# Taking absolute values of float64 weight words on ScalarE two pieces ahead and on VectorE, with the cells of steps 2 and 3 in another hand order

## Chip, cores and metric

The kernel runs on one core of a Trainium2 chip. The metric is the time of one execution on the device in microseconds (us). Engines are called PE (TensorE), DVE (VectorE), ACT (ScalarE), POOL (GpSimd) and SP (SyncE, which only issues transfers here).

## What is computed

An mLSTM cell runs over 4 batches x 8 heads x 768 positions with a head size of 40, and its output (3072 tokens x 320) goes through a feed-forward block: `h = x @ w_in` (320 x 2048), `g = max(0.01 h, h)`, `out = g @ w_out` (2048 x 320).

```python
m_new = maximum(f + m, i);  C = exp(f + m - m_new) * C + exp(i - m_new) * v k^T   # per head, per position
h = C q;  y = sigmoid(o) * h / max(|n q|, 1)
g = maximum(0.01 * (x @ w_in), x @ w_in);  out = g @ w_out
```

The two weight matrices come in as float64 and have to be narrowed to float32 on the core. q, k, v and the gates are float32.

## The kernel before

**Tiling.** The 768 positions are cut into 6 chunks of 128. A *step* `s` is one chunk of one batch (24 steps, chunk `s // 4`, batch `s % 4`). The *cell* of a step consists of a few functions, each of which issues the work of several engines: `u_transpose` (k and q transposed on PE, copied to `kqT` by ACT from step 2 on, L331), `u_scores` (PE `sc` L340, then two DVE multiplications L344), `u_state` (PE `pc` L354 and `dC` L365), `u_values` (PE `pa` L384, then on DVE the denominators L389 to L393), `gate` (DVE L402, then POOL L405, which gives `x`), and `u_x` (PE transposes `x`, ACT copies it to `xT`). `prep_exp` holds eight exponentials on ACT (L301), `prep_o` a tanh on ACT (L316), `prep_mask` a POOL addition (L291), `prep_vu` a POOL multiplication (L309).

**Feed-forward.** `ff_units(g)` gives the feed-forward of chunk `g` as a list of units. For chunk 0 these are 8 units of `half` over the first 256 columns of `xT` (call them ff0 to ff7), 8 over the second 256, and 16 of `part`, which multiply by `w_out` (PE `po`, L474). A `half` unit is 8 matmul records at L430, 4 at L436, and two activations on ACT (L444). Unit ff*j* needs piece *j* of `w_in`. The 16 `part` units go in four rounds, one unit per batch each: round 0 needs pieces 8 and 9, round 1 pieces 10 and 11, and so on.

**Narrowing.** Each matrix is cut into 8 pieces of 128 x 640 values: pieces 0 to 7 are `w_in`, 8 to 15 `w_out`. `load_weights` brings a piece as 64-bit words into a buffer `raw` (6 of them). `narrow_weights(n)` then makes float32 of it: the absolute value of the high word (ACT, L155, in `absolute`), and six DVE instructions, L170, L174, L178, L180, L182 and L189. The high word is read with a stride of 8 bytes. It is a generator which yields after each DVE instruction, and `narrow(k)` issues the next `k` of them, whatever piece they belong to.

**Where the absolute value is issued.** For piece 0 and for every piece of `w_out` it comes right ahead of that piece's own L170; for pieces 1 to 7 it comes ahead of L189 of the piece before.

**What sets the order.** On PE, DVE, ACT and POOL the order of the instructions is the order in which the program issues them (`manual_schedule`): each engine works through its own queue, and waits at an instruction until its inputs are there. `first_chunk` is an order written by hand, with calls of `narrow` between cells and units. After it, a loop runs over the units of chunk 0 that are left (i = 0 to 23) and spreads the cells of chunk 1 between them from i = 6 on; from i = 4 on it calls `narrow(3)` ahead of each unit. At i = 5 it issues `u_gates(1)` and `ahead(4)` (POOL, ACT and POOL work for step 4), at i = 6 `gates(2)` (six DVE instructions L206 to L226, then ACT L219 and L220). On the SP queue a scheduler picks the order of the transfers.

Of the kernel before, what the change touches and what calls it, by code (L numbers as in the profile page):

```python
# [13 lines left out]
ALU = mybir.AluOpType  # L14
# [4 lines left out]
def kernel(  # L19
# [26 lines left out]
    nc = tc.nc  # L46
# [66 lines left out]
    NP = NF // 2  # L113
# [39 lines left out]
    def absolute(n):  # L153
        lo, hi, dst = raws[n]
        nc.scalar.activation(dst, hi.bitcast(F32), AF.Abs)  # L155

    def narrow_weights(n):

        if not wide:
            return
        if n == 0 or n >= NP:
            absolute(n)
        lo, hi, dst = raws.pop(n)
        mt = wk.tile([P, dst.shape[1]], U32, name="wm", bufs=1)
        m = mt[:]
        d = dst.bitcast(U32)

        nc.vector.tensor_scalar(  # L170
            m.bitcast(F32), dst, scalar1=2.0**-15, scalar2=122879.9921875, op0=ALU.max, op1=ALU.min,
        )
        yield
        nc.vector.tensor_scalar(  # L174
            m, m, scalar1=0x07FFFFFF, scalar2=3, op0=ALU.bitwise_and, op1=ALU.logical_shift_left,
        )
        yield
        nc.vector.scalar_tensor_tensor(d, in0=hi, scalar=0xC0000000, in1=m, op0=ALU.bitwise_and, op1=ALU.bitwise_or)  # L178
        yield
        nc.vector.tensor_scalar(m, d, scalar1=0xFF800000, scalar2=None, op0=ALU.bitwise_and)  # L180
        yield
        nc.vector.scalar_tensor_tensor(  # L182
            m.bitcast(F32), in0=lo, scalar=2.0**-52, in1=m.bitcast(F32), op0=ALU.mult, op1=ALU.mult,
        )
        yield
        if n + 1 < NP:

            absolute(n + 1)
        nc.vector.tensor_tensor(dst, dst, m.bitcast(F32), op=ALU.add)  # L189
        yield  # L190

# [101 lines left out]
    def prep_exp(s):  # L293

        c, b = divmod(s, B)
        if c == 0:
            w = st[s]["w"] = wk.tile([P, H, P], F32, name="w", bufs=NL)
        w = st[s]["w"]
        for h in range(H):
            bh = b * H + h  # L300
            nc.scalar.activation(w[:, h, :], w[:, h, :] if c > 0 else st[s]["ab"][h], AF.Exp, bias=gT[:, c, 0, bh : bh + 1], scale=1.0)  # L301
# [12 lines left out]
    def prep_o(s):  # L314

        nc.scalar.activation(st[s]["o"][:], st[s]["o"][:], AF.Tanh, scale=0.5)  # L316


    def u_transpose(s):
        d = st[s]  # L320
        d["kqT"] = wk.tile([P, 2, PR, P], F32, name="kqT")
        for i in range(2):
            tp = psc.tile([P, PR, P], F32, name="tkq", tag="c")
            for j in range(PR):
                nc.tensor.transpose(  # L325
                    tp[:, j, :], d["kq"][:, i, 2 * j : 2 * j + 2, :].rearrange("p h d -> p (h d)"), ident[:],
                )
            if s < 2:
                nc.vector.tensor_copy(d["kqT"][:, i], tp[:])
            else:  # L330
                nc.scalar.copy(d["kqT"][:, i], tp[:])  # L331

    def u_scores(s):
        d = st[s]
        kqT, w = d["kqT"], d["w"]
        sc = [psc.tile([P, PR, P], F32, name=f"sc{r}", tag="c") for r in range(2)]
        for j in range(PR):
            for r in range(2):
                rows = slice(DP * r, DP * r + D)
                nc.tensor.matmul(  # L340
                    sc[r][:, j, :], lhsT=kqT[rows, 0, j, :], rhs=kqT[rows, 1, j, :], start=True, stop=True,
                )
        for r in range(2):
            nc.vector.tensor_tensor(w[:, r::2, :], w[:, r::2, :], sc[r][:], op=ALU.mult)  # L344
# [52 lines left out]
    def gate(s):  # L397

        d = st[s]
        d["x"] = wk.tile([P, Dm], F32, name="x")  # L400
        x3 = d["x"][:].rearrange("p (h d) -> p h d", d=D)
        nc.vector.scalar_tensor_tensor(  # L402
            x3, in0=d["o"][:], scalar=1.0, in1=d["hn"][:, :, :D], op0=ALU.add, op1=ALU.mult,
        )
        nc.gpsimd.tensor_tensor(x3, x3, d["den"][:].unsqueeze(2).to_broadcast([P, H, D]), op=ALU.mult)  # L405

    def u_x(s):

        c, b = divmod(s, B)
        d = st[s]  # L410
        if b == 0:
            st["xT", c] = wk.tile([P, KF + 1, GT], F32, name="xT")
        xT = st["xT", c]
        xt = psc.tile([P, KF + 1, P], F32, name="xt", tag="c")
        for kk in range(KF):
            nc.tensor.transpose(xt[:, kk, :], d["x"][:, ts(kk, P)], ident[:])  # L416
        nc.tensor.transpose(xt[:KR, KF, :], d["x"][:, KF * P :], ident[:])
        nc.scalar.copy(xT[:, :KF, ts(b, P)], xt[:, :KF, :])
        for r in range(2):
            nc.scalar.copy(xT[KR * r : KR * (r + 1), KF, ts(b, P)], xt[:KR, KF, :])  # L420
        del st[s]
# [100 lines left out]
    def narrow(count):  # L522
        for _ in range(count):
            next(narrowing, None)

    def first_chunk():

        load(0)
        load(1)
        load_weights(0)  # L530
        load_o(0)
        load_o(1)
        for n in range(1, 5):
            load_weights(n)
        load(2)
        load_weights(5)
        load_weights(6)
        load_weights(7)
        load(3)
        load_o(2)  # L540
        load_o(3)
        load_weights(NP)
        load_weights(NP + 1)
        ab = mask_first((0, 1), (0, 1, 2, 3))
        bu, a = gates(0)
        gates_T(0, bu)
        spread_first(a, ab, (0, 1))
        prep_exp(0)
        u_transpose(0)
        prep_vu(0)  # L550
        u_scores(0)
        prep_exp(1)
        u_state(0)
        u_transpose(1)
        prep_vu(1)
        u_values(0)
        u_scores(1)
        u_state(1)
        narrow(2)
        prep_o(0)  # L560
        gate(0)
        narrow(1)
        u_values(1)
        prep_o(1)
        gate(1)
        narrow(3)
        u_x(0)
        u_x(1)
        ffs = ff_units(0)
        ffs[0]()  # L570
        narrow(6)
        ab = mask_first((2,), (0, 2))
        spread_first(a, ab, (2,))
        ffs[1]()
        prep_exp(2)
        narrow(6)
        ffs[2]()
        narrow(6)
        ab = mask_first((3,), (0, 2))
        spread_first(a, ab, (3,))  # L580
        ffs[3]()
        prep_exp(3)
        narrow(6)
        u_transpose(2)
        prep_vu(2)
        ffs[4]()
        u_scores(2)
        narrow(3)
        u_state(2)
        narrow(3)  # L590
        u_values(2)
        ffs[5]()
        prep_o(2)
        narrow(3)
        gate(2)
        u_transpose(3)
        prep_vu(3)
        narrow(3)
        u_x(2)
        u_scores(3)  # L600
        ffs[6]()
        narrow(3)
        u_state(3)
        u_values(3)
        prep_o(3)
        gate(3)
        narrow(3)
        ffs[7]()
        u_x(3)
        return ffs[8:]  # L610

    E = mybir.EngineType
    with tc.manual_schedule(engines={E.PE, E.DVE, E.Activation, E.Pool}):
        ffs = first_chunk()
        bus[1] = gates(1)
        feed(B)
        load_weights(NP + 2)
        load_weights(NP + 3)
        feed(B + 1)
        load_weights(NP + 4)  # L620
        load_weights(NP + 5)
        feed(B + 2)
        load_weights(NP + 6)
        load_weights(NP + 7)
        feed(B + 3)
        for c in range(1, NB + 1):
            if c > 1:
                ffs = ff_units(c - 1)
            cells = cell_units(c) if c < NB else []
            n_ff, n_c = len(ffs), len(cells)  # L630
            lead = 6 if c == 1 else 0
            done = 0
            for i in range(n_ff):
                if c == 1 and i >= 4:
                    narrow(3)
                if c == 1 and i == 5:
                    u_gates(1)
                    ahead(B)
                if i == lead and c + 1 < NB:
                    bus[c + 1] = gates(c + 1)  # L640
                ffs[i]()
                upto = min(n_c, max(0, i + 1 - lead) * n_c // (n_ff - 3 - lead))
                while done < upto:
                    fn, s = cells[done]
                    fn(s)
                    done += 1
                    if fn is u_transpose:
                        ahead(s + 1)
                    elif fn is u_values and s + NL < NS:
                        feed(s + NL)  # L650
# [31 lines left out]
```

## Time and profile before

| | |
|---|---|
| three timed runs | 641.93, 640.20, 641.08 us (median 641.08) |
| the profiled execution | span 641.0 us, mean granted PE clock 0.963 |
| PE busy | 610.6 us, 95% of the span |
| DVE, ACT, POOL busy | 177.9, 184.7 and 102.1 us |
| L155 on ACT | 16 times, about 0.79 us each |

The page gives one execution. A row such as `L474 PE MATMUL po<-w_out,act ... x768 | 224.6, 444` reads: 768 instructions of line 474, 224.6 us in all, 444 ns each on average. PE's share of 95% is an average over a start in which PE waits and a long rest in which it doesn't, so the stages have to be looked at apart.

### The profile page before, as it was taken

Reading aid. Unit: us, or ns where it says so; the run is one execution under the profiler, and the core shown is the slowest. Engines: PE = TensorE matmul, PEld = TensorE weight load, DVE = VectorE, ACT = ScalarE, POOL = GpSimd, SP = SyncE. Lnnn points to the kernel's source line nnn. Section 1 sums busy time; section 2 is a strip of 40 time slices with the busy share of each in tenths; the row PEclk is TensorE's granted clock in tenths of the full one; section 3 lists DMA queues with packets and bytes.
Section 4 is the critical chain, followed back from the end, with each engine's and each line's share of the span. In section 5 each row is a group of like instructions: output and inputs, shape, how many; then the busy total and the mean of one; then the engine's idle time right before and its main releaser. Section 6 shows DMA issues by size and latency. Waiting matters only on the chain.

```text
span 641.0 us, 7844 instructions
## 1 busy us (share of the span) xinstructions
PE 610.6 (95%) x3062; PEld 388.7 (61%) x3062; DVE 177.9 (28%) x367; ACT 184.7 (29%) x505; POOL 102.1 (16%) x110
## 2 busy tenths in 40 slices
PE   8888697988899999999999999999999999999997
PEld 5656565766655557755557755557754467743475
DVE  4774606687622111222111222111201111100000
ACT  4333335322342341232441232441222441012200
POOL 3200112323122022022022021022011010000000
PEclk9597899897999999999999999999999999999999
DMA  9996442433233023133123122123120000000000
GB/s 166 235 214 174 97 170 66 102 75 65 42 86 72 13 64 77 46 70 59 26 63 77 44 70 56 30 64 75 43 61 2 0 1 15 17 11 0 1 20 21
DMA packets 112692, 41.51 MB, mean 65 GB/s; under 512 B 101424, under 2 KB 105936, under 8 KB 112656
## 3 DMA queue, kind: packets, MB, share of 16 engines
q1 hardware_dynamic: 112368, 40.79, 27.7%
q8 instruction: 24, 0.39, 0.2%
q10 hardware_dynamic: 288, 0.23, 0.2%
q14 instruction: 12, 0.10, 0.1%
HBM read 37.00 MB, written 4.01 MB: 64 GB/s over the span
## 4 chain that ended last, share of the span: by engine, by line
PE 84%; DVE 8%; ACT 4%; POOL 2%; issue 1%; POOLq 0%; DVEq 0%; ACTq 0%
PE po L474 29%; PE ph L430 27%; PE ph L436 8%; PE pa L384 7%; PE sc L340 4%; PE tkq L325 3%; PE pc L354 2%; ACT w L301 2%; PE dC L365 1%; PE ab L267 1%; DVE wm L182 1%; POOL w L291 1%; PE xt L416 1%; DVE w L344 1%; DVE w_in L189 1%
## 5 line engine op out<-in xcount | busy, mean ns | idle before, releaser
L474 PE MATMUL po<-w_out,act 128*128 128x320 f32 x768 | 224.6, 444 | 3.2 <-DVE w_out L189 3.2
L430 PE MATMUL ph<-xT,w_in 128*128 128x512 f32 (+1 forms) x448 | 190.4, 563 | 8.1 <-DVE w_in L189 7.2
L474 PEld LDWEIGHTS po<-w_out,act 128*128 128x128 f32 x768 | 143.3, 193 | 59.8 <-DVE w_out L189 4.2
L430 PEld LDWEIGHTS ph<-xT,w_in 128*128 128x128 f32 x448 | 84.3, 201 | 77.2 <-issue 59.3
L444 ACT ACTIVATE act<-ph 128x512 f32<-128x512 f32 (+1 forms) x112 | 53.9, 534 | 175.6 <-PE ph L436 175.6
L405 POOL TENSOR_TENSOR x<-x,den 128x320 f32<-128x320 f32 x24 | 18.6, 773 | 421.5 <-DVE x L402 421.5
L344 DVE TENSOR_TENSOR w<-w,sc 128x512 f32<-128x512 f32 x48 | 30.8, 683 | 186.9 <-PE sc L340 186.9
L436 PE MATMUL ph<-xT,w_in 64*128 64x512 f32 (+1 forms) x224 | 58.0, 595 | 0.0
L384 PEld LDWEIGHTS pa<-va,w 128*128 128x128 f32 x384 | 50.2, 207 | 10.3 <-issue 5.2
L384 PE MATMUL pa<-va,w 128*128 128x41 f32 x384 | 51.0, 295 | 2.5 <-DVE w L344 2.4
L479 ACT COPY y<-po 128x320 f32<-128x320 f32 x24 | 10.2, 423 | 147.1 <-PE po L474 85.2
L301 ACT ACTIVATE w<-w,gT 128x128 f32<-128x128 f32 x160 | 49.0, 399 | 11.4 <-POOL w L291 8.8
L291 POOL TENSOR_TENSOR w<-w,cmask 128x1024 f32<-128x1024 f32 x20 | 48.5, 2425 | 9.2 <-DMA w<-a_dr 9.2
L331 ACT COPY kqT<-tkq 128x512 f32<-128x512 f32 x44 | 23.7, 597 | 77.2 <-PE tkq L325 77.2
L436 PEld LDWEIGHTS ph<-xT,w_in 64*128 64x128 f32 x224 | 17.5, 191 | 36.8 <-issue 36.8
L340 PEld LDWEIGHTS sc<-kqT 40*128 40x128 f32 x384 | 24.4, 193 | 16.7 <-ACT kqT L331 8.8
L340 PE MATMUL sc<-kqT 40*128 40x128 f32 x384 | 28.6, 289 | 5.9 <-ACT kqT L331 5.0
L386 DVE TENSOR_TENSOR hn<-hn,pa 128x328 f32<-128x328 f32 x20 | 9.9, 496 | 70.0 <-PE pa L384 70.0
L325 PEld LDWEIGHTS tkq<-ident,kq 128*128 128x128 f32 x192 | 21.9, 143 | 11.4 <-issue 9.8
L358 DVE TENSOR_TENSOR hn<-pc,gT 128x328 f32<-128x328 f32 x20 | 10.0, 498 | 58.6 <-PE pc L354 58.6
L325 PE MATMUL tkq<-ident,kq 128*128 128x128 f32 x192 | 26.1, 280 | 0.0
L354 PEld LDWEIGHTS pc<-C,kqT 128*128 128x128 f32 x160 | 20.8, 192 | 7.0 <-issue 5.1
(70 smaller groups left out, 333.5 us busy)
## 6 DMA issues: line engine op xcount, KB each, us to landing
w<-a_dr SPq DMA_DIRECT2D x20, 512.0 KB, 5.0
raw<-in_moe_w_out_dram SPq DMA_DIRECT2D x8, 640.0 KB, 5.0
raw<-in_moe_w_in_dram SPq DMA_DIRECT2D x16, 256.0 KB, 4.2
kq<-in_k_dram SPq DMA_DIRECT2D x24, 160.0 KB, 2.8
kq<-in_q_dram SPq DMA_DIRECT2D x24, 160.0 KB, 3.3
va<-in_v_dram SPq DMA_DIRECT2D x24, 160.0 KB, 2.8
o_sb<-in_o_gate_dram SPq DMA_DIRECT2D x24, 160.0 KB, 4.6
out_dram<-y SPq DMA_DIRECT2D x24, 160.0 KB, 1.8
```

Source lines behind the costliest of these rows:

```text
L291: nc.gpsimd.tensor_tensor(w[:], w[:], cmask[:].unsqueeze(1).to_broadcast([P, H, P]), op=ALU.add)
L301: nc.scalar.activation(w[:, h, :], w[:, h, :] if c > 0 else st[s]["ab"][h], AF.Exp, bias=gT[:, c, 0, bh : bh + 1], scale=1.0)
L325: nc.tensor.transpose(tp[:, j, :], d["kq"][:, i, 2 * j : 2 * j + 2, :].rearrange("p h d -> p (h d)"), ident[:],)
L331: nc.scalar.copy(d["kqT"][:, i], tp[:])
L340: nc.tensor.matmul(sc[r][:, j, :], lhsT=kqT[rows, 0, j, :], rhs=kqT[rows, 1, j, :], start=True, stop=True,)
L344: nc.vector.tensor_tensor(w[:, r::2, :], w[:, r::2, :], sc[r][:], op=ALU.mult)
L354: nc.tensor.matmul(pc[:, 2 * j : 2 * j + 2, :].rearrange("p h d -> p (h d)"), lhsT=d["kqT"][:, 1, j, :], rhs=C[:, b, j].rearrange("p h d - ...
L384: nc.tensor.matmul(pa[:, h, :], lhsT=d["w"][:, h, :], rhs=d["va"][:, h, :], start=True, stop=True)
L430: nc.tensor.matmul(ph[:, cols], lhsT=w_full(kk, f), rhs=xT[:, kk, cols], start=(kk == 0), stop=False,)
L436: nc.tensor.matmul(ph[r][:, cols], lhsT=w_rest(r, j), rhs=xT[KR * r : KR * (r + 1), KF, cols], start=False, stop=True,)
L444: nc.scalar.activation(acts[f][:, cols], ph[r][:, cols], AF.Prelu, alpha=0.01)
L474: nc.tensor.matmul(po[n][:], lhsT=acts[f][:, ts(n, P)], rhs=w_out[:, f, :], start=(f == 0), stop=(f == NF - 1),)
```

## The change

Three edits, all of them in the narrowing and in the hand order:

1. For `w_in`, the absolute value of piece n + 2 is now issued ahead of L189 of piece n (before: piece n + 1), and that of piece 1 between L174 and L178 of piece 0. It stays on ACT.
2. For `w_out` the absolute value is now a DVE instruction, a bitwise AND with 0x7FFFFFFF on the high word, and a step of its own: a piece of `w_out` has seven steps in place of six. The loop calls `narrow(4)` in place of `narrow(3)`.
3. In `first_chunk`, the cells of steps 2 and 3 and the calls of `narrow` stand in another order.

```diff
-        if n == 0 or n >= NP:
-            absolute(n)
+        if n == 0:
+            absolute(0)
...
+        if n >= NP:
+            nc.vector.tensor_scalar(d, hi, scalar1=0x7FFFFFFF, scalar2=None, op0=ALU.bitwise_and)
+            yield
...
+        if n == 0:
+            absolute(1)
         nc.vector.scalar_tensor_tensor(d, in0=hi, scalar=0xC0000000, in1=m, op0=ALU.bitwise_and, op1=ALU.bitwise_or)
...
-        if n + 1 < NP:
-
-            absolute(n + 1)
+        if n + 2 < NP:
+
+            absolute(n + 2)
         nc.vector.tensor_tensor(dst, dst, m.bitcast(F32), op=ALU.add)
...
-        narrow(3)
+        narrow(2)
         u_x(0)
         u_x(1)
+        narrow(1)
         ffs = ff_units(0)
...
         narrow(6)
         ffs[2]()
-        narrow(6)
         ab = mask_first((3,), (0, 2))
         spread_first(a, ab, (3,))
-        ffs[3]()
-        prep_exp(3)
         narrow(6)
         u_transpose(2)
         prep_vu(2)
+        ffs[3]()
+        prep_exp(3)
+        narrow(3)
+        u_scores(2)
+        narrow(3)
+        u_state(2)
+        u_values(2)
         ffs[4]()
-        u_scores(2)
-        narrow(3)
-        u_state(2)
-        narrow(3)
-        u_values(2)
+        prep_o(2)
+        narrow(3)
+        gate(2)
+        narrow(3)
         ffs[5]()
-        prep_o(2)
-        narrow(3)
-        gate(2)
+        u_x(2)
         u_transpose(3)
         prep_vu(3)
         narrow(3)
-        u_x(2)
         u_scores(3)
+        narrow(3)
+        u_state(3)
         ffs[6]()
         narrow(3)
-        u_state(3)
         u_values(3)
         prep_o(3)
+        narrow(3)
         gate(3)
-        narrow(3)
         ffs[7]()
         u_x(3)
...
                 if c == 1 and i >= 4:
-                    narrow(3)
+                    narrow(4)
```

In the order of the compiled program, the PE instructions from the end of ff2 on to ff8, the first unit of the second half, stand like this:

| | order on PE |
|---|---|
| before | step 3's mask, ff3, transpose 2, ff4, scores 2, state 2, values 2, ff5, transpose 3, x 2, scores 3, ff6, state 3, values 3, ff7, x 3, ff8 |
| after | step 3's mask, transpose 2, ff3, scores 2, state 2, values 2, ff4, ff5, x 2, transpose 3, scores 3, state 3, ff6, values 3, ff7, x 3, ff8 |

After ff8 PE's order is the same in both. POOL's order is the same throughout. On DVE the w_out pieces 8 to 15 have eight instructions more, and with four steps ahead of each unit in place of three they stand earlier against the cells. On ACT eight L155 are gone from the part after ff8. On SP a few transfers change places with their neighbours (the loads of w_out pieces 10 to 14 and of the steps 4 to 8); none is added and none taken away.

More of the change, by code (lines that the diff above doesn't have):

```diff
@@ L585, in first_chunk @@
         prep_vu(2)
-        ffs[4]()
+        ffs[3]()
+        prep_exp(3)
+        narrow(3)
         u_scores(2)
@@ L589, in first_chunk @@
         u_state(2)
-        narrow(3)
         u_values(2)
-        ffs[5]()
+        ffs[4]()
         prep_o(2)
@@ L595, in first_chunk @@
         gate(2)
+        narrow(3)
+        ffs[5]()
+        u_x(2)
         u_transpose(3)
```

## The prediction
> **What bounds the kernel now.** I read the slices of the page first (PE's clock and share fall below 9 tenths only among the first eleven of 40), then cut the span into four stages: up to ff8, up to the end of scores 4, up to the transposes of x 7, and the rest. Busy time of each engine by stage, with the granted PE clock after it:
>
> ```profile
> core 0: us, PE busy (x) PEld busy (x) DVE busy (x) ACT busy (x) POOL busy (x), PEclk, DMA share, GB/s
> 0.00:84.80 84.80, 70.33 (x417) 49.02 (x417) 48.98 (x94) 29.27 (x86) 11.16 (x22) 0.80 0.79 178
> 84.80:112.70 27.90, 23.97 (x126) 17.09 (x126) 9.70 (x20) 13.18 (x41) 7.11 (x6) 0.95 0.37 111
> 112.70:176.70 64.00, 56.31 (x351) 43.03 (x350) 46.65 (x80) 19.37 (x53) 18.90 (x17) 0.91 0.33 70
> 176.70:641.00 464.30, 459.98 (x2170) 279.59 (x2170) 72.54 (x174) 122.84 (x327) 64.93 (x66) 1.00 0.18 41
> ```
>
> The last stage is PE at full clock without gaps, and the change touches nothing there: 464.3 us stay. Everything is decided in the first 177 us, where PE idles and runs at a reduced clock. Next the waits between 84 and 177 us (who waited for whom, sum, times, longest):
>
> ```profile
> DVE wm L170 <- ACT w_out L155: 29.9, 6, 15.4
> PE sc L340 <- ACT kqT L331: 3.9, 1, 3.9
> PE po L474 <- DVE w_out L189: 3.2, 2, 2.5
> ```
>
> DVE waits 29.9 us for absolute values on ACT that themselves take 0.79. Then the timeline (start, duration, engine, in brackets the idle time before and its releaser):
>
> ```profile
> 65.79 0.49 DVE L402 SCALAR_TENSOR_TENSOR x<-o_sb,pa 128x320 f32<-128x320 f32 x1 [3.81 <-ACT o_sb L316]
> 79.65 3.53 PE L430 MATMUL ph<-xT,w_in 128*128 128x256 f32 x8 [3.65 <-DVE w_in L189]
> 104.14 0.79 ACT L155 ACTIVATE w_out<-raw 128x640 f32<-128x640 f32 x1
> 104.96 0.50 DVE L170 TENSOR_SCALAR wm<-w_out 128x640 f32<-128x640 f32 x1 [4.05 <-ACT w_out L155]
> 108.48 0.40 ACT L219 ACTIVATE bu<-bu,a 32x128 f32<-32x128 f32 x1 [3.56 <-DVE bu L218]
> 110.60 2.15 PE L340 MATMUL sc<-kqT 40*128 40x128 f32 x16 [3.92 <-ACT kqT L331]
> 112.68 4.50 PE L474 MATMUL po<-w_out,act 128*128 128x320 f32 x8
> 120.37 2.40 PE L474 MATMUL po<-w_out,act 128*128 128x320 f32 x8
> 123.03 2.93 POOL L291 TENSOR_TENSOR w<-w,cmask 128x1024 f32<-128x1024 f32 x1
> 123.78 2.87 DVE L189 TENSOR_TENSOR w_out<-w_out,wm 128x640 f32<-128x640 f32 x1
> 134.79 1.34 PE L474 MATMUL po<-w_out,act 128*128 128x320 f32 x4 [2.50 <-DVE w_out L189]
> 150.16 0.41 PE L384 MATMUL pa<-va,w 128*128 128x41 f32 x2 [1.84 <-DVE w L344]
> ```
>
> The reader is to see a ring at 104 to 113: L155 stands on ACT behind the exponentials of step 4, DVE waits for it with gates(2) queued behind, ACT then waits for gates(2), the copy of kqT behind that is late, and PE idles 3.92 us. Scores 4 and the next eight `po` then run at half rate (2.15 for 1.16 us, 4.50 for 2.40). The last rows show the gaps of the third stage, and one thing to remember: an L189 of 0.82 us takes 2.87 beside a POOL mask.
>
> [...] ff5 runs slow at 59.78 (3.78) behind a gap of 0.83. [...] The trace: L170 0.49, L189 0.82 for the same 640 elements. [...]
>
> **The change part by part.** Start-to-start on DVE: 0.52 for L170, L174, L180 and 0.86 for L178, L182, L189, 4.1 a piece.
>
> *Removed and added.* Eight L155 leave ACT after ff8: 8 x 0.79 = 6.3 us, off the path except through DVE's waits. DVE gets eight ANDs. No row shows a tensor_scalar with an 8-byte stride; the bounds are L170 (0.49) and L178, which reads the same strided words at 0.82. I take 0.52; the other end adds 0.33 each, 2.6 in all. A cost below 0.49 is excluded, since L170 moves as many elements.
>
> *Stage 1, to ff8 (edits 1 and 3).* Up to 42.9 PE doesn't move: the masks of step 3 wait for the exponentials of step 2 (end 39.6) in both orders. Pieces 2 and 3 no longer wait for ACT (1.79 and 3.85 us of DVE idle): they run from 30.5 to 38.7, before: to 44.4. PE: transposes 2 to 43.8, ff3 (2.6) to 46.4 at full clock, scores 2 to 47.5. DVE: L344 twice to 48.9, the last three steps of piece 4 (2.2) to 51.1, where ff4 starts. Before, that first L344 pair ended at 55.7, so this is 6.8 us ahead. But the new order has ff5 behind ff4 with nothing between, and piece 5 stands on DVE behind gate(2), which needs a tanh that stands on ACT behind ff4's activations. Before, from such activations (64.74) over tanh, L402 and three steps to the next unit (69.27) took 4.5: ff4 ends at 53.8, ff5 starts at 58.3, with PE idle 4.5. At half rate ff5 takes 4.6 (62.9), x 2 and transposes 3 1.7, copies 1.1, scores 3 1.1, L344 1.3, three steps 2.2: ff6 at 70.3. It takes 4.3, pa 3 1.9 (76.5), denominators and three steps 2.8: ff7 at 79.3, before 79.65. The lead is spent on one more round of PE waiting for DVE waiting for PE: -0.4. If ff4 too runs at half rate (as ff5 did at 59.78; even odds) 2.8 come on top. I take **+1.0**; range -4.2 (ff5 and ff6 at full clock, 1.9 each) to +2.4.
>
> *Stage 2, ff8 to the first `po` (edit 2).* Piece 8 needs no ACT now: its seven steps fit into DVE's idle time after gates(1) (15.38 us before L170 at 96.5). So gT is copied when PE has it, at 98.2 instead of 100.6. Behind it stand four steps of piece 9 (2.4), the hold by step 5's mask (2.3, as with the 2.87) and gates(2) (1.6): 104.5. ACT: L219 and L220 0.7, activations 0.6, kqT 1.0: scores 4 at 106.8, where PE arrives at 106.3. Idle 3.9 becomes 0.5 (-3.4), scores 4 at full clock -1.0, the first `po` -2.1: **-6.5**; range -2 to -7.
>
> *Stage 3, to the transposes of x 7.* Losses of before: 2.50, 1.84 + 0.18 and 0.72 of idle, `pa` 6 slow (3.4 for 2.0), the `po` at 153.54 slow (4.54 for 2.40): 8.7. The 2.46 us for x 7 on DVE and POOL stay. But DVE fills up: from the end of L344 for step 4 (109.3) to x 5 its queue holds piece 10's rest, pieces 11 and 12 and an AND (13.5), cells 4 and 5 (6.7), the wait for pa 4 (0.6) and the hold by POOL (3.3): L402 ends at 133.4, POOL's L405 at 134.4. PE gets there at 131.3, so it idles 3.1, a new wait in place of the old; behind the waiting L386 on DVE stand piece 13's steps. Another 1.0 comes before pa 6 (L344 behind piece 14's first steps). -8.7 + 4.1 = -4.6, and even odds of 2 us of half rate behind the new gap: **-3.6**; range -8.7 to 0.
>
> SP: piece 14's load waits for piece 8's L182, 15's for piece 9's; both come earlier, so no transfer is later. POOL keeps its order. ACT, busy for 19.4 of the 64 us of stage 3, has room.
>
> Sum against the profiled span, 641.0 (the runs: 640.2 to 641.9): 641.0 + 1.0 - 6.5 - 3.6 = **631.9**.
>
> **Rivals.**
> A, DVE keeps up: the ANDs aren't held by POOL's masks, and the gap before x 5 closes: 641.0 - 0.4 - 6.5 - 8.7 = 625.4. For it: an L180 beside POOL's L405 took 0.49 (122.00). Against: an L174 beside it took 0.90.
> B, the start gives back more: half rate in ff4 (+1.4 on my mean), ANDs at 0.85 (+2.6), and stage 2 half gained (+1.5): 637.4. For it: the clock of 0.80 over stage 1.
> C, slower: [...] If DVE, now without idle time, is held for all of POOL's work in a cell (0.84 + 2.93 + 1.31 + 0.99 = 6.1 us) instead of 2.5, three cells cost 3 x 3.6 more, and step 5's mask in stage 2 2.7: 645.3. It decides from 5.4 us a cell on. Against: beside L309 and L374 an L182 took 1.24, not 3.
> That the change isn't what it says can be left out: the compiled order shows the L155 gone and the ANDs there.
>
> **How the numbers follow.** Forecast 0.50, A 0.20, B 0.22, C 0.08. About 0.3% (1.9 us) is what this measurement can tell from no change: faster is below 639.1. Forecast and A lie there, B with 0.17 of its 0.22, 0.05 of it within: faster 0.87, same 0.05, slower 0.08. The range 624.5 to 638.0 leaves out C and the outer ends of A and B, 0.2 together.
>
> **What would show it.** Right: no idle time of DVE behind L155 after ff8; scores 4 with under 1 us of idle before it and 1.16 long; ff7 near 79; PE idle before x 5's transposes, released by POOL L405. Wrong: ff8 off 84.5 by over 3 us; an AND above 0.6; scores 4 still waiting for kqT over 2 us; DVE idle between 110 and 130.

## The result and the profile after

The changed kernel takes **634.57 us** (median of four runs, 632.59 to 635.08), the kernel before 640.64 on the same chip (639.69 to 641.93). The ratio is 0.9898, with a 95% interval of 0.9869 to 0.9927: about 1% faster. The profiled execution has a span of 632.9 us, where that of before has 641.0. In both the time of the execution is 2.0 us above its span (634.99 and 643.0).

All lines of the changed kernel stand about five higher than in the kernel before: L189 is now L194, L316 is L321, L331 is L336, L405 is L410, L474 is L479. The new AND is L170, and the instruction that was L170 is L173.

The stages first. For each window: its length, the busy time of the engines with their instructions, PE's granted clock, the DMA share. The cuts are ff8, the end of the first eight `po`, and the transposes of x 7.

```profile
core 0: us, PE busy (x) PEld busy (x) DVE busy (x) ACT busy (x) POOL busy (x), PEclk, DMA share, GB/s
0.00:86.10 86.10, 66.97 (x417) 46.61 (x417) 52.48 (x100) 29.12 (x86) 10.64 (x22) 0.80 0.83 173
86.10:112.60 26.50, 25.31 (x134) 17.90 (x135) 13.30 (x23) 12.93 (x42) 8.30 (x6) 1.00 0.41 134
112.60:167.00 54.40, 49.75 (x343) 38.93 (x341) 47.97 (x81) 14.09 (x43) 20.02 (x17) 0.97 0.37 78
167.00:632.90 465.90, 461.67 (x2170) 280.65 (x2170) 72.53 (x174) 122.84 (x327) 64.87 (x66) 1.00 0.18 40
```

With the same cuts the kernel before has 84.8, 32.2, 59.7 and 464.3 us; its second and third stage:

```profile
84.80:117.00 32.20, 28.27 (x133) 19.93 (x134) 12.80 (x25) 14.93 (x45) 7.11 (x6) 0.89 0.34 104
117.00:176.70 59.70, 52.01 (x343) 40.19 (x341) 43.55 (x75) 17.61 (x48) 18.90 (x17) 0.94 0.35 71
```

The change is +1.3, -5.7, -5.3 and +1.6: the gain lies in the second and third stage, and the first and last give some of it back. Between ff8 and x 7 PE's clock is now 1.00 and 0.97 (before: 0.89 and 0.94).

The waits between 84 and 170 us (who waited for whom: sum, times, longest) no longer hold the row that stood out before, DVE for L155 with 29.9 us. What DVE still waits for is PE, and PE's own waits are small:

```profile
DVE gT L242 <- PE tg L239: 12.0, 1, 12.0
...
PE xt L421 <- POOL x L410: 4.7, 2, 2.5
...
PE sc L345 <- ACT kqT L336: 1.1, 1, 1.1
```

The 12.0 us at L242 hold nothing up on PE. But four steps of piece 9 stand behind L242 in DVE's queue, and from 117 to 159 us DVE has no idle time left; whether steps issued ahead of L242 would pay later was not tried.

The timeline (start, duration, engine, in brackets the idle time before and its releaser):

```profile
49.75 1.97 PE L435 MATMUL ph<-xT,w_in 128*128 128x256 f32 x8 [0.46 <-DVE den L394]
53.43 0.49 DVE L407 SCALAR_TENSOR_TENSOR x<-o_sb,pa 128x320 f32<-128x320 f32 x1 [1.56 <-ACT o_sb L321]
57.00 3.75 PE L435 MATMUL ph<-xT,w_in 128*128 128x256 f32 x8 [4.65 <-DVE w_in L194]
68.85 3.78 PE L435 MATMUL ph<-xT,w_in 128*128 128x256 f32 x8 [2.90 <-DVE w_in L194]
73.72 3.64 PE L389 MATMUL pa<-va,w 128*128 128x41 f32 x16
80.20 3.78 PE L435 MATMUL ph<-xT,w_in 128*128 128x256 f32 x8 [2.85 <-DVE w_in L194]
101.29 2.87 DVE L183 SCALAR_TENSOR_TENSOR w_out<-raw,wm 128x640 uint32<-128x640 uint32 x1
109.17 1.23 PE L345 MATMUL sc<-kqT 40*128 40x128 f32 x16 [1.15 <-ACT kqT L336]
110.33 2.42 PE L479 MATMUL po<-w_out,act 128*128 128x320 f32 x8
118.29 1.02 DVE L170 TENSOR_SCALAR w_out<-raw 128x640 uint32<-128x640 uint32 x1
118.92 2.61 POOL L296 TENSOR_TENSOR w<-w,cmask 128x1024 f32<-128x1024 f32 x1
119.34 2.54 DVE L173 TENSOR_SCALAR wm<-w_out 128x640 f32<-128x640 f32 x1
132.89 0.48 DVE L170 TENSOR_SCALAR w_out<-raw 128x640 uint32<-128x640 uint32 x1
135.94 0.44 PE L421 MATMUL xt<-ident,x 128*128 128x128 f32 x2 [2.20 <-POOL x L410]
136.33 4.01 PE L479 MATMUL po<-w_out,act 128*128 128x320 f32 x8
167.63 8.07 PE L479 MATMUL po<-w_out,act 128*128 128x320 f32 x24
```

The reader is to see four things. *The start*: ff4 at 49.75 runs at full rate, and then PE stands still for 4.65, 2.90 and 2.85 us ahead of ff5, ff6 and ff7, waiting for DVE; all three (3.75, 3.78 and 3.78 for 1.99), and pa 3 between them, run at half rate (3.64 for 1.98). *The ring*: the wait ahead of scores 4 is 1.15 us instead of 3.92, and what follows is at full rate. *DVE*: an AND takes 0.48 alone and 1.02 beside POOL's work, and beside each of the POOL masks of steps 5 to 8 one DVE instruction, an L173 as well as an L183, lasts until shortly behind the mask's end (2.54 for 0.49 and 0.35 us behind it, 2.87 for 0.83 and 0.68 behind it). *The new wait*: PE waits 2.20 us for x 5, and the eight `po` after it take 4.01 instead of 2.32. In the last row 24 `po` take 8.07, behind the same wait of 2.46 us for x 7 as before; that is nearly all of the 1.6 us of the last stage. The kernel before:

```profile
177.09 6.62 PE L474 MATMUL po<-w_out,act 128*128 128x320 f32 x24
```

### The profile page after: what moved, and what is told of

Same layout as the page of the kernel before. It is cut to its first block, busy times and chain, and to the rows that moved or that the text cites. A ratio compares the mean times of both kernels' runs of the same rounds, so it can differ in the third digit from the quotient of the medians.

```text
span 632.9 us, 7836 instructions
## 1 busy us (share of the span) xinstructions
PE 603.7 (95%) x3062; PEld 384.1 (61%) x3062; DVE 186.3 (29%) x375; ACT 179.0 (28%) x497; POOL 103.8 (16%) x110
## 3 DMA queue, kind: packets, MB, share of 16 engines
HBM read 37.00 MB, written 4.01 MB: 65 GB/s over the span
## 4 chain that ended last, share of the span: by engine, by line
PE 86%; DVE 8%; SPq 2%; ACT 1%; issue 1%; POOL 1%; DMA 1%; POOLq 0%; DVEq 0%; ACTq 0%
PE po L479 31%; PE ph L435 28%; PE ph L441 8%; PE pa L389 6%; PE sc L345 4%; PE tkq L330 3%; PE pc L359 3%; PE dC L370 1%; DVE wm L187 1%; PE xt L421 1%; SPq L252 1%; DVE w_in L194 1%; SPq L144 1%; PE ab L272 1%; DVE wm L185 1%
## 5 line engine op out<-in xcount | busy, mean ns | idle before, releaser
L479 PE MATMUL po<-w_out,act 128*128 128x320 f32 x768 | 223.0, 442 | 0.0
L435 PE MATMUL ph<-xT,w_in 128*128 128x512 f32 (+1 forms) x448 | 189.7, 562 | 12.5 <-DVE w_in L194 11.1
L479 PEld LDWEIGHTS po<-w_out,act 128*128 128x128 f32 x768 | 143.2, 192 | 55.7 <-issue 2.9
L435 PEld LDWEIGHTS ph<-xT,w_in 128*128 128x128 f32 x448 | 83.7, 200 | 81.5 <-issue 62.5
L410 POOL TENSOR_TENSOR x<-x,den 128x320 f32<-128x320 f32 x24 | 19.1, 797 | 414.6 <-DVE x L407 414.6
L389 PEld LDWEIGHTS pa<-va,w 128*128 128x128 f32 x384 | 47.5, 197 | 9.0 <-issue 5.9
L296 POOL TENSOR_TENSOR w<-w,cmask 128x1024 f32<-128x1024 f32 x20 | 48.1, 2403 | 7.5 <-DMA w<-a_dr 7.5
L389 PE MATMUL pa<-va,w 128*128 128x41 f32 x384 | 48.2, 286 | 0.8 <-DVE w L349 0.8
L336 ACT COPY kqT<-tkq 128x512 f32<-128x512 f32 x44 | 23.7, 594 | 73.3 <-PE tkq L330 73.3
```

The lines of the kernel that those rows point to most:

```text
L296: nc.gpsimd.tensor_tensor(w[:], w[:], cmask[:].unsqueeze(1).to_broadcast([P, H, P]), op=ALU.add)
L389: nc.tensor.matmul(pa[:, h, :], lhsT=d["w"][:, h, :], rhs=d["va"][:, h, :], start=True, stop=True)
L435: nc.tensor.matmul(ph[:, cols], lhsT=w_full(kk, f), rhs=xT[:, kk, cols], start=(kk == 0), stop=False,)
L479: nc.tensor.matmul(po[n][:], lhsT=acts[f][:, ts(n, P)], rhs=w_out[:, f, :], start=(f == 0), stop=(f == NF - 1),)
```

## The experiments

Eleven kernels were run. Each ratio is to the kernel before on the same chip (medians 641.55 for kernels 1 to 4, 640.98 for 5 to 8 and 641.43 us for 9 to 11). The lines shown of kernels 3, 4, 5, 7 and 9 have the numbers of the changed kernel; its L435 is L433 in kernel 1 and L432 in kernels 2, 6, 8, 10 and 11, and likewise for the others.

| kernel | median us | ratio | 95% interval |
|---|---|---|---|
| the change | 634.57 | 0.9898 | 0.9869 to 0.9927 |
| 1 edit 2 alone | 631.56 | 0.9855 | 0.9829 to 0.9881 |
| 2 edits 1 and 3 | 643.84 | 1.0024 | 1.0009 to 1.0038 |
| 3 the change, x 5 first | 636.20 | 0.9922 | 0.9900 to 0.9945 |
| 4 the change, tanh first | 630.83 | 0.9827 | 0.9809 to 0.9845 |
| 5 the change, four masks left out | 630.52 | 0.9828 | 0.9801 to 0.9856 |
| 6 all absolute values ahead on ACT | 624.85 | 0.9746 | 0.9717 to 0.9774 |
| 7 edits 1 and 2, old hand order | 627.84 | 0.9793 | 0.9767 to 0.9819 |
| 8 as 6, tanh first | 623.19 | 0.9724 | 0.9699 to 0.9749 |
| 9 the change, idle time filled | 629.65 | 0.9815 | 0.9795 to 0.9834 |
| 10 as 8, piece 7 earlier | 617.81 | 0.9625 | 0.9607 to 0.9643 |
| 11 as 10, idle time filled | 617.11 | 0.9620 | 0.9600 to 0.9640 |

The theory was the prediction's: the gain comes from the ring and the stage behind it, through edit 2; the hand order of edit 3 spends its lead on PE waiting for DVE waiting for PE. The rival gave the hand order a part in the gain, or put the loss of DVE elsewhere.

### 1: edit 2 alone, in the order of before

```diff
-        if n == 0 or n >= NP:
-            absolute(n)
+        if n == 0:
+            absolute(0)
...
+        if n >= NP:
+            nc.vector.tensor_scalar(d, hi, scalar1=0x7FFFFFFF, scalar2=None, op0=ALU.bitwise_and)
+            yield
...
-                    narrow(3)
+                    narrow(4)
```

> Edit 2 alone: the hand order and the absolute values of w_in are those of the kernel before, only the absolute values of w_out go to DVE, with four steps ahead of each unit. Theory (edit 2 carries the gain, the new hand order gives 1 to 2.5 us back in stage 1): ff8 starts as in the kernel before (84.8 us, give or take 1), scores 4 has about 1 us of idle before it, and the time is 1 to 2.5 us below the changed kernel, 632 to 633.5. Rival (the new hand order is worth something, hidden in the profile by half-rate phases): slower than the changed kernel, 636 to 639.

631.56 us: edit 2 alone gives at least as much as the whole change; its median is lower, but the two intervals just overlap. Its waits ahead of scores 4 and x 5 are those of the changed kernel:

```profile
104.60 1.23 PE L343 MATMUL sc<-kqT 40*128 40x128 f32 x16 [1.15 <-ACT kqT L334]
...
131.38 0.69 PE L419 MATMUL xt<-ident,x 128*128 128x128 f32 x2 [2.20 <-POOL x L408]
```

One part of the expectation missed: ff8 starts at 81.58 and not near 84.8. Of these 3.2 us this execution was 2.2 ahead at ff2 already, and ff6 runs at full rate (1.99, before: 3.59). Nothing that the edit touches stands there.

### 2: edits 1 and 3, absolute values of w_out on ACT as before

```diff
-        if n == 0:
-            absolute(0)
+        if n == 0 or n >= NP:
+            absolute(n)
...
-            nc.vector.tensor_scalar(d, hi, scalar1=0x7FFFFFFF, scalar2=None, op0=ALU.bitwise_and)
-            yield
...
-                    narrow(4)
+                    narrow(3)
```

> Edits 1 and 3 alone: new hand order and w_in's absolute values two pieces ahead, but w_out's absolute values stay on ACT ahead of each piece, with three steps ahead of each unit. Theory: stage 1 as in the changed kernel (ff8 at 86, PE idle 4.5 us before ff5 and 2.9 before ff6 and ff7), then the ring of the kernel before (3.9 us of idle before scores 4, half rate behind it): 641.5 to 643, not faster than the kernel before. Rival (the hand order gains by itself): 634 to 639.

643.84 us, slightly slower than before and above the range expected. In its waits view DVE's row for L155 stands as it did (29.0 us), and its timeline has the start of the changed kernel and the ring of the old one:

```profile
56.99 3.75 PE L432 MATMUL ph<-xT,w_in 128*128 128x256 f32 x8 [4.65 <-DVE w_in L191]
...
111.92 1.74 PE L342 MATMUL sc<-kqT 40*128 40x128 f32 x16 [3.93 <-ACT kqT L333]
```

So the whole gain of the change is edit 2's. What edit 1 brings (kernels 1 and 7 differ by it, 0.9855 and 0.9793, about 4 us) is lost by edit 3 in the same stage.

### 3: x 5 ahead of the narrowing

```diff
-                    narrow(4)
+                    narrow(0 if i == 12 else 8 if i == 13 else 4)
```

> The changed kernel with four narrowing steps (2.8 us on DVE) moved from ahead of step 5's x to behind it: no step ahead of unit i = 12, eight ahead of i = 13. Theory (DVE has no idle time left from 110 to 158 us, so a wait that is taken away there comes back at the next place where PE needs DVE): the 2.2 us of PE idle before x 5 and the half rate behind it (1.6 us) go, but pa 6 now waits about 2 us for L349; gain 0 to 2 us against the changed kernel, 632.5 to 634.5. Rival (the wait for x 5 is local): both go and nothing comes back, 3.8 us, 630 to 631.

636.20 us, not faster than the change (the intervals overlap), where a gain of up to 2 us was expected. The wait ahead of x 5 is gone, and it has moved as the theory said, though with a higher price:

```profile
132.25 0.38 PE L421 MATMUL xt<-ident,x 128*128 128x128 f32 x2
...
142.46 3.81 PE L389 MATMUL pa<-va,w 128*128 128x41 f32 x16 [2.68 <-DVE w L349]
146.07 3.75 PE L479 MATMUL po<-w_out,act 128*128 128x320 f32 x8
```

PE waits 2.68 us for the DVE multiplications of the next cell, and `pa` 6 and the `po` behind it run at half rate. DVE has no idle time to give in this stretch: a step put back in one place is missing in the next.

### 4: the tanh of step 2 ahead of ff4

```diff
-        ffs[4]()
-        prep_o(2)
+        prep_o(2)
+        ffs[4]()
```

> The changed kernel with the tanh of step 2 (prep_o) issued ahead of ff4 in place of behind it, so that on ACT it stands ahead of ff4's two activations. Theory (PE's idle 4.65 us before ff5 is the round ff4, activations, tanh, L407, three steps of piece 5): L407 no longer waits 1.56 us, the idle before ff5 shrinks to about 3.1 us and ff8 comes 1.5 us earlier; 632 to 633.5. Rival (the tanh's place doesn't matter, DVE's queue of narrowing steps sets ff5): idle before ff5 stays at 4.5 us or more, 634 to 635.

630.83 us, a larger gain than expected:

```profile
54.44 1.97 PE L435 MATMUL ph<-xT,w_in 128*128 128x256 f32 x8 [3.00 <-DVE w_in L194]
...
64.21 3.78 PE L435 MATMUL ph<-xT,w_in 128*128 128x256 f32 x8 [2.90 <-DVE w_in L194]
```

The idle time ahead of ff5 falls by 1.65 us to 3.00, as the chain tanh, gate(2), piece 5 wanted it; that part of the step is shown. But ff5 also runs at full rate, which is worth two more. A gap of 2.90 us ahead of ff6 is still followed by half rate: the length of the gap alone doesn't decide.

### 5: POOL's masks of steps 5 to 8 left out

The causal mask isn't added in these four steps, so part of the computation is missing.

```diff
-            prep_mask(s)
+            if s not in (5, 6, 7, 8):
+                prep_mask(s)
```

> The changed kernel without POOL's causal mask additions (L296) of steps 5 to 8: those four steps' weights are left unmasked, so the output differs there; everything else is the same. It measures what POOL's masks cost DVE. Theory (each mask holds one DVE instruction for about 2.5 us, and DVE is full from 100 to 158 us): DVE has about 2 us of idle time before L407 of step 5, the idle before scores 4 falls from 1.15 us to under 0.5, the wait for x 5 (2.2 us) and the half rate behind it go: 4 to 6 us below the changed kernel, 629 to 631. Rival (the holds fall into time that DVE has to spare): the same as the changed kernel within 1 us, 634 to 636.

630.52 us, 4 below the change and within the range expected. The wait ahead of x 5 is almost gone, and the units behind it are at full rate:

```profile
133.43 0.44 PE L421 MATMUL xt<-ident,x 128*128 128x128 f32 x2 [0.16 <-POOL x L410]
133.81 2.32 PE L479 MATMUL po<-w_out,act 128*128 128x320 f32 x8
```

So the masks are what makes DVE late for x 5: in the changed kernel's trace each of the four goes with one DVE instruction that lasts 2.03 to 2.05 us longer than alone. POOL's other work in a cell, which was left in, doesn't do it alone (0.16 us of wait remain).

### 6 and 7: the old hand order, w_out's absolute values on ACT or on DVE

Both keep the hand order of before and issue w_in's absolute values two pieces ahead (edit 1). In kernel 7 those of w_out are the ANDs of edit 2. In kernel 6 they stay on ACT, two pieces ahead as well; there is no AND, and the loop stays at `narrow(3)`:

```diff
-        if n == 0 or n >= NP:
-            absolute(n)
+        if n == 0:
+            absolute(0)
...
+        if n == 0:
+            absolute(1)
...
-        if n + 1 < NP:
-            absolute(n + 1)
+        if n + 2 < 2 * NP:
+            absolute(n + 2)
```

> The kernel before with only the place of the absolute values changed: two pieces ahead for all sixteen pieces, all of them on ACT; hand order and narrow(3) as before, no AND on DVE. It tells whether the gain comes from the other engine or from the earlier place. Theory (DVE's waits for ACT are what counts, and DVE has no room for the eight ANDs): DVE waits nowhere for L155 after ff8, scores 4 has under 1.2 us of idle before it, there is no wait before x 5, and the time is below that of the edit 2 alone (631.6): 626 to 630. Rival (ACT is too full, its own queue delays kqT and the exponentials by the 0.79 us that each L155 takes): 632 to 636.

> Edits 1 and 2 with the hand order of the kernel before (edit 3 undone). Theory: w_in's absolute values ahead take the 1.6 us of idle before ff3 and the half rate behind it away, which the hand order of the changed kernel then loses again: 1.5 to 3 us below edit 2 alone, 628.5 to 630. Rival (edit 1 pays only together with the new order): as edit 2 alone, 631 to 632.5.

624.85 and 627.84 us, both below the changed kernel and by about 1 us below the ranges expected. Kernel 7 differs from it by edit 3 alone. The two ratios, 0.9793 and 0.9898, put that edit at about 6.7 us of loss. The trace finds the same: from the start of ff2 to ff8 kernel 7 takes 43.3 us (37.25 to 80.56), the changed kernel 49.9 (36.26 to 86.14). Kernel 7's PE:

```profile
51.81 3.81 PE L389 MATMUL pa<-va,w 128*128 128x41 f32 x16 [0.18 <-DVE w L349]
56.45 3.78 PE L435 MATMUL ph<-xT,w_in 128*128 128x256 f32 x8 [0.83 <-DVE w_in L194]
...
65.95 1.99 PE L435 MATMUL ph<-xT,w_in 128*128 128x256 f32 x8 [0.32 <-DVE w_in L194]
...
74.72 3.78 PE L435 MATMUL ph<-xT,w_in 128*128 128x256 f32 x8 [3.64 <-DVE w_in L194]
```

Here ff4 stands ahead of scores 2 and ff6 ahead of values 3, so that PE has a unit to do while DVE works; ff5 and ff6 wait 0.83 and 0.32 us instead of 4.65 and 2.90, while ff7 waits 3.64 instead of 2.85. The new order isn't bound to lose all of it: kernel 4 keeps it and gets some 4.6 of the 6.7 us back by the place of one tanh (0.9827 and 0.9898), about two of them by the rate of ff5, which is partly luck (see below).

Kernel 6 has no AND at all, and DVE has no wait for L155 left after ff8 either. The waits at scores 4 (0.76) and at `po` (0.35) are small, and the one ahead of x 5 is absent:

```profile
103.56 1.23 PE L342 MATMUL sc<-kqT 40*128 40x128 f32 x16 [0.76 <-ACT kqT L333]
...
128.59 0.38 PE L418 MATMUL xt<-ident,x 128*128 128x128 f32 x2
```

The masks are the same here, but DVE has eight instructions less, and one step less ahead of each unit. Its interval just overlaps that of kernel 7, so that the 3 us between them are likely rather than certain. What is certain is that the AND isn't needed: the ring opens when the absolute value stands early enough in ACT's queue.

### 8: kernel 6 with the tanh of step 2 ahead of ff5

```diff
-        ffs[5]()
-        prep_o(2)
+        prep_o(2)
+        ffs[5]()
```

> e6_act_ahead with the tanh of step 2 issued ahead of ff5 in place of behind it (in this hand order ff5 stands where ff4 stands in the changed kernel). Theory: L402 of step 2 no longer waits 3.8 us for the tanh, ff6 starts 1 to 1.5 us earlier: 1 to 3 us below e6_act_ahead. Rival: kqT of step 3, which stands behind ff5's activations on ACT, sets ff6 anyway: within 0.7 us of e6_act_ahead.

623.19 us against 624.85; the direction is the expected one, the intervals overlap. The wait of 1.06 us ahead of the transposes of x 2 is gone in the trace; one of 0.40 for kqT ahead of scores 3 has come, so that the rival has a part in it.

### 9: the changed kernel with PE's idle time filled

```diff
+    def warm(count):
+        t = psf.tile([P, GT], F32, name="warm", tag="mm")
+        for _ in range(count):
+            nc.tensor.matmul(t[:, :PC], lhsT=ident[:], rhs=w_in[:, 0, :PC], start=True, stop=True)
...
+        warm(14)
         ffs[5]()
...
+        warm(8)
         ffs[6]()
...
+        warm(8)
         ffs[7]()
```

> The changed kernel with matmuls ahead of ff5, ff6 and ff7 (14, 8 and 8 of 128 x 256, into a tile that nobody reads) that fill PE's idle time there. Theory: PE runs at half rate because it stood idle before, and the losses behind the three gaps (ff5 1.8 + 0.3, ff6 1.8 + 0.5, pa 3 1.7, ff7 1.8 + 0.5, all on the path to ff8: 8.4 us) are mostly regained: 6 to 8.5 us under the changed kernel, 626.5 to 629. Rival: the rate is set by something else than the idle time (or the filling matmuls only stand in the way): no gain, 634 to 637, ff5, ff6 and ff7 still about 3.75.

629.65 us: about 5 below the change, where 6 to 8.5 were expected.

```profile
51.70 6.31 PE L534 MATMUL warm<-w_in,ident 128*128 128x256 f32 x28
57.85 1.89 PE L435 MATMUL ph<-xT,w_in 128*128 128x256 f32 x8
...
70.59 1.98 PE L389 MATMUL pa<-va,w 128*128 128x41 f32 x16
...
129.26 0.44 PE L421 MATMUL xt<-ident,x 128*128 128x128 f32 x2 [2.20 <-POOL x L410]
...
129.64 2.32 PE L479 MATMUL po<-w_out,act 128*128 128x320 f32 x8
```

ff5, ff6 and ff7 (1.89 each) and pa 3 (1.98) all run at full rate: with PE's idle time filled, their half rate is gone, so the idle time is what brought it. That idle time always does so doesn't follow: in kernel 4 ff5 kept full rate (1.97) behind 3.00 us. The fillers were too many ahead of ff5 (6.31 us for a gap of 4.65, so that ff5 comes 1.4 us later after ff4 than it did), and yet from ff4 to ff8 the kernel takes 30.3 us instead of 36.4. From ff8 to the end it takes 1.6 more (548.3 against 546.8): the `po` at 139.28 are slow (3.96 for 2.40) and so are the 24 behind x 7 (8.99 for 6.62), the ones behind x 5 are not.

### 10 and 11: piece 7 earlier, and with fillers

Kernel 10 is kernel 8 with the last three steps of piece 7 moved ahead of values 3; kernel 11 adds three filling matmuls ahead of scores 2 and two ahead of ff5.

```diff
         ffs[6]()
-        narrow(3)
+        narrow(6)
...
         gate(3)
-        narrow(3)
         ffs[7]()
```

> The run with all absolute values two ahead on ACT and the tanh of step 2 ahead of ff5, and in it the last three narrowing steps of piece 7 moved ahead of values 3 instead of behind gate(3). Theory: the 3.65 us of PE's idle time ahead of ff7 are those three steps behind the denominators; they fit into 2.06 us of idle DVE before, so ff7 starts right behind pa 3 and runs at full rate: 3 to 6 us under the run without this (623.2), 617 to 620. Rival: the lead is given back at scores 4 or at x 5: 622 to 624.

> The same with three filling matmuls ahead of scores 2 and two ahead of ff5. Theory (half rate follows even gaps of about 1 us): pa 2 (3.81 for 1.98) and ff5 (3.78 + 1.23 for 2.7) return to full rate, and of these 4.1 us 1.5 to 3 reach the end, since piece 6 on DVE binds next: 1.5 to 3 us under the run without the fillers. Rival (a gap of 1 us has no part in it): within 0.7 us of that run, pa 2 and ff5 still at half rate.

617.81 and 617.11 us, both 3.8% below the kernel before. In kernel 10 the gap ahead of ff7 closes and its half rate goes with it; in kernel 8 this unit stood at 71.39 with 3.65 of idle time and took 3.78:

```profile
68.45 1.99 PE L432 MATMUL ph<-xT,w_in 128*128 128x256 f32 x8 [0.35 <-DVE w_in L191]
```

In kernel 11 pa 2 (14 of the 16 in 1.75, where all 16 took 3.81 in kernel 10) and ff5 (1.97 for 3.78) return to full rate, and ff8 starts 2.1 us sooner after ff0 than in kernel 10 (45.5 against 47.5). But behind x 7 the 24 `po` take 9.03 us instead of 7.85, and the span is only 0.4 shorter. The medians differ by 0.7 us where 1.5 to 3 were expected. The fillers bring back the rate as the theory said; that they are worth it at the end isn't shown.

## Why the prediction was right, and where its sizes were off

Against its own span the sum came out at 631.9, and the span was 632.9. The timed median, 634.57, is higher because the time of the execution was 2.0 us above its span (634.99 and 632.9). The prediction set the span of 641.0 beside runs of 640.2 to 641.9 as if the two were one quantity; the profiled execution of before (643.0) was itself 2 us above the median of its kernel, and that hid the difference. A change of 9.1 us was predicted, 8.1 shows between the two traces and 6.1 between the medians. All lie in the range. The sum is closer than its terms: the third stage gained 1.7 us more than predicted and the last lost 1.6 more, and that the two nearly cancel is luck.

**The ring (right).** The prediction put most of the gain on L155 in ACT's queue. Kernel 2 puts it back and has the wait of 3.93 us again, kernel 1 takes it out alone, and kernel 6 takes it out with L155 still on ACT. Stage 2 was put at -6.5 and measured -5.7: the term that was off is the idle time ahead of scores 4, 0.5 predicted and 1.15 measured. The hold by step 5's mask was priced well (2.0 us of loss, 2.3 in the sum); four other instructions beside POOL's work were not priced (0.91 twice for 0.49, 0.67 for 0.40, 0.41 for 0.25, together 1.3 us) and brought gates(2) later. The sum has PE at scores 4 at 106.3; the trace of before gives 106.7 (110.60 less 3.92 of idle time), so that the idle time should have come out at 0.1 and was missed by more than it seems.

**The price of an AND (right).** 0.52 start to start was taken, and 0.52 was measured in free stretches (each 0.47 to 0.49 long). The dearer end of the bounds, 0.85 for each, didn't come. Two of the eight, though, took 1.02 and 1.01 beside POOL's work, above the 0.6 that the prediction named as a sign of being wrong.

**The start (right, with a wrong term).** +1.0 was predicted and +1.3 measured, and the idle time ahead of ff5, worked out as 4.5, was 4.65. But this run came to ff2 1.0 us earlier than the one before, so that the stretch in the new hand order, from ff2 to ff8, takes 2.3 more (49.9 for 47.5). The early start is chance: kernels 3, 4 and 5, which are the same program up to there, came to ff2 at 35.33, 35.34 and 37.29 (the change: 36.26, before: 37.28). So the close match of +1.0 and +1.3 is luck. The even odds of half rate were put on ff4, which ran at full rate; instead pa 3 (3.64 for the 1.9 used) and the close of ff6 and ff7 were slow. From ff6 to ff7 the prediction has 9.0 us, and the trace 11.35. Kernel 9 shows what this term was: idle time followed by half rate, priced at one place by chance and in truth present at three.

**The third stage (too cautious).** -3.6 predicted, -5.3 measured. The new wait ahead of x 5 came where it was put, released by POOL's L405 of before, but was 2.20 instead of 3.1: from the two multiplications of step 4 to the end of L407 of step 5 DVE took 23.2 us, not 24.1. The hold in it, 3.3 with the instructions around it, was right. The second, 1.0 ahead of pa 6, didn't come. The half rate behind the gap did (4.01 for 2.32, so 1.7 where even odds made it 1.0). Kernel 5 shows the cause of the wait.

**The last stage (missed).** 0 was predicted, +1.6 measured. The wait for x 7 is the old one, 2.46, but the `po` behind it are slower. Nothing in the program changed there. The 24 `po` took 7.8 to 9.2 us in nine other traces (the change and kernels 1 to 4, 6 and 9 to 11), and 6.62 in that of before alone. Kernel 2, which has the ring of before and no gain, reaches x 7 at 176.61, before at 176.71, and there the 24 take

```profile
176.99 8.32 PE L476 MATMUL po<-w_out,act 128*128 128x320 f32 x24
```

So the 1.6 us aren't a cost of the change: the trace of before was lucky at this gap. The step of the prediction that failed is that the 464.3 us of this stage stay whatever happens; how the gap falls in time (next paragraph) moves them.

**The rivals.** A (DVE keeps up) is refuted: the wait for x 5 stayed. C (POOL holds DVE through a whole cell) too: DVE lost about 2 us a cell in the held instruction and 3.3 with those around it, where C decides from 5.4 on. B was right that the start gives back more than the walk alone, by the rate of PE, but not on the ANDs nor on stage 2.

**When PE falls to half rate (settled in part by the traces).** The prediction's ff5 of before at 59.78, slow behind 0.83 us, doesn't show what a gap brings, since PE was slow ahead of that gap already (14 of the 16 `pa` 2, which take 1.76 us in the changed kernel):

```profile
55.74 3.21 PE L384 MATMUL pa<-va,w 128*128 128x41 f32 x14 [0.18 <-DVE w L344]
```

The traces record PE's granted clock. In those of before and of the change it is 1.00 or 0.50, and it stays at one of the two for 3.41 us (136.40 to 139.81 in the change, at 0.50) or for a whole multiple of that (85.20 to 136.40, at 1.00, is fifteen times as long), so that all its changes lie on one grid; its first line stands at 0.87 us of the span in before and at 3.28 in the change. The table cuts the time along the grid, for gaps ahead of which the clock was 1.00; the gap's part in a stretch stands beside the time for which PE was busy there:

| gap of PE | its part in each stretch of 3.41 us (PE busy) | clock in the stretch after it |
|---|---|---|
| the change, x 5, 2.20 us | 2.20 (1.21) | 0.50 |
| the change, x 7, 2.46 us | 2.46 (0.95) | 0.50 |
| before, x 7, 2.46 us | 0.69 (2.72) and 1.77 (1.65) | 1.00 and 1.00 |
| before, `po` at 134.79, 2.50 us | 1.69 (1.71) and 0.80 (2.61) | 1.00 and 1.00 |
| before, pa 6, 1.84 and 0.18 us | 2.03 in all (1.38) | 0.50 |

The two gaps ahead of x 7 have the same length. The one that lies whole in a stretch is followed by half rate, the one that falls into two stretches is not, and neither is the 2.50 us; the shorter gaps ahead of x 5 and pa 6 lie whole in one stretch and are. So in these rows the place of a gap against the grid goes with what its length doesn't tell. Kernels 4 and 9 have gaps of 3.00 and 2.20 us behind which PE kept full rate (1.97 for ff5, 2.32 for the `po` behind x 5); where the grid lay there isn't shown here. At the start too the stretches at half rate differ: before is at 0.50 from 17.93 to 31.59 us and comes to ff2 at 37.28, the change from 20.35 to 30.59 and comes there at 36.26.

**What stays open.** How little work in a stretch brings half rate: no single limit comes out of these traces, since in before a stretch with the 1.63 us of the gap ahead of ff3 (PE busy for 1.78) was followed by 0.50, and the one with 1.77 ahead of x 7 (PE busy for 1.65) by 1.00. The first line of the grid differs between the two traces, and the time of one program from execution to execution: the 22 executions of kernel 2 have spans from 638.4 us at a mean granted clock of 0.968 to 643.5 at 0.957. Differences of a few us between kernels that were executed four to six times are to be read with that in mind; the 6 to 17 us by which the main steps differ from the kernel before are beyond it. No run placed a gap against the grid on purpose.

## What to carry to other kernels

When an engine waits for a short operation at the end of another engine's queue, first try to issue that operation earlier where it is: here the same opening of the ring cost nothing on ACT and eight instructions on a DVE that then had none to spare. An order in which two units of the bounding engine stand back to back, with their next inputs behind each other on a helper engine, gives back what was won: keep a unit between any two steps of such a loop, or shorten the loop itself, as kernel 4 did with the tanh. And price a gap of PE with the half rate that may follow it (here 4.01 us instead of 2.32 for eight `po` behind 2.20 us), since filling the gaps of the changed kernel, which left their time in place, gained some 5 us (kernel 9).

## What the runs showed of the hardware that was not expected

In the trace of the change seven POOL additions of 128 x 1024 (L296) each held one DVE instruction until 0.28 to 0.68 us behind their own end, and those after it ran at a moderate loss: behind the L173 of 2.54 us stand an L177 of 0.91 and an L183 of 0.97 (alone 0.49 and 0.83). Which instruction is held, an L173 (2.53 and 2.54 for 0.49), an L183 (2.86 and 2.87 for 0.83) or an L217 (2.47 and 2.48 for 0.41), makes little difference: 2.0 to 2.1 us are lost each time. Not every instruction is held: beside three other additions (at 241.03, 337.35 and 433.67) the copies L242 and L243 took 0.26 and 0.18 us, as they did at 99.56 with no addition beside them.

Work without use can pay: in kernel 9 thirty matmuls that nobody reads (60 records in the trace), in all three places longer than the gap they fill, brought the next units to full rate and the kernel some 5 us. The gain isn't certain to stay, since later gaps then fall differently: kernel 11 lost half of its 2.1 us again behind x 7.
